# A fifth seven-product block pair in five tiles, strided heads in halves, and a new order of steps and outputs

## The chip, the cores and the metric

The kernel runs on one core of one Trainium2 chip. The metric is the device time of one execution in microseconds (us); for several runs their median is given. The engines are named as in the profile: PE is the matrix engine (TensorE), PEld its weight loads, DVE is VectorE, ACT is ScalarE, POOL is GpSimd, and SP is the queue of SyncE, which here only issues DMAs.

## The reference

Eight heads of sparse attention over 8 batches of 576 tokens; heads 0 to 3 see the last 32 tokens ("local"), heads 4 to 7 see every 32nd token ("strided"). Its output, 4608 tokens of 512 features, goes through a bilinear feed-forward layer.

```python
batch, n_heads, seq, head_dim = (8, 8, 576, 64)
mask_local = (rel >= 0) & (rel < stride)                       # stride = 32
mask_strided = (rel >= 0) & (pos[None, :] % stride == pos[:, None] % stride)
...
attn = np.exp(scores)
attn = attn / (np.sum(attn, axis=-1, keepdims=True) + 1e-09)
attn_out = np.matmul(attn, v)
...
a = x @ w_a            # (4608 x 512) @ (512 x 1536)
b = x @ w_b
return (a * b @ w_out) # (4608 x 1536) @ (1536 x 512)
```

## The kernel before

**Tiles and slots.** The feed-forward layer works on nine tiles of 512 tokens, numbered t = 0 to 8 in the code; tiles "3 to 7" are t = 2 to 6, and these are the ones that the dictionary `MID_A` names. A tile has 16 slots. In slots 0 to 11 the twelve 128-wide blocks f of the hidden layer are made (`a = x @ w_a`, `b = x @ w_b`, product into the buffer `pf`), in slots 12 to 15 ("Y") the output rows. Blocks go in six pairs g = f // 2. A plain block is eight matmuls of 512 columns (four for a, four for b; `ab_mm`, L625), an ACT copy of a out of PSUM (L646) and a DVE multiply with b (L649).

**Pairs by seven products.** For pairs 1 to 4 of t = 2 to 6, `a_pair_mid` computes the a halves of both blocks by seven block products (a 2 x 2 block scheme) in place of eight. Each product is two matmuls of 256 columns (`P`, L695). It needs sums of weights, `wsum_make` (L668, made once), and of inputs, `xsum_make` (L678, once a tile). The order inside a pair is: product 2 into bank Y; product 1 into bank X, which ACT then copies out (`q00`, L721); three of the four matmuls of the second block's b ("b1", L709); product 6 added into X, copied out again (`q10`, L724); product 7 into Z, copied (`p7`, L726); the last b1 matmul; DVE adds Y to `q00` (L717). Here the first half, the even slot, ends. In the odd slot: product 5 added into X, copied (`q11`, L731); product 4 added into Z, DVE adds Z to `q10`; four matmuls of the other b ("b0"); DVE adds `p7` to `q11`; product 3 added into X, copied (`q01`, L738); DVE multiplies both blocks (L714). X is thus written four times and copied four times, and each product on X after the first waits until the copy before it has read the bank. The banks are the four of the rotation `mm_bank` and a fifth, "e"; which of them is X, Y, Z, b1 and b0 follows from (g - 1) % 3.

**Output.** `y_plan` makes the output rows by seven products as well: 84 matmuls of 256 columns (L895), six for each letter and parity in the order `Y_ORDER` (10 11 70 71 ... : product, then token parity 0 or 1). They use three banks X, Y, Z; when a product's second parity ends, `y_post` copies the bank out on ACT (L860) or adds it on DVE. The sums of `pf` that products 3, 5, 6 and 7 read are made by `fast_s` on DVE (L829; n = 0 to 3).

**Attention.** The steps of batch b = t + 1 are put by hand between the matmuls of tile t: `PAIRED` gives steps after a slot, `IN_P` inside the second half of a pair just ahead of the add of `p7`, `IN_Y` after an output product. A step "s4" is the score matmuls of unit 4 into the bank pair `st` (L379) and their exponential on ACT (L399); "m4" is the mask on DVE (L417); "S" is both. "V" is the product with v: for units 0 to 3 (local) L460 with a reciprocal and a multiply on DVE; for units 4 to 7 (strided) `step_VT`: four matmuls into bank "o" and four into "e" (L519), two Ln on ACT (L531), one Exp (L532), two DVE multiplies into `xT` (L534), which is the input of the feed-forward layer. "Q" copies transposed queries (L335), "O" and "I" send rows of the local heads through memory and back, transposed.

**What sets the order.** All five queues are in program order; nothing reorders the instructions. POOL and SP issue the loads and stores; a one-element copy `pace` (L1146) holds POOL's queue to the slots.

Of the kernel before, what the change touches and what calls it, by code (L numbers as in the profile page):

```python
# [7 lines left out]
F32 = mybir.dt.float32  # L8
# [8 lines left out]
RS = 8  # L17
# [8 lines left out]
LV = 80  # L26
WCH = (0, 2, 5, 9, 12)
FAST_Y = (1, 2, 3, 4, 5, 6, 7, 8)
MID_A = {t: (1, 2, 3, 4) for t in (2, 3, 4, 5, 6)}
FAST_A = {7: (1, 2, 3, 4, 5), 8: (0, 1, 2, 3, 4, 5)}  # L30


# [1 line left out]
def kernel(  # L34
# [138 lines left out]
    def fast_w(n, gs):  # L173
        a, b = ((wov[:, 0, 1], wov[:, 0, 0]), (wov[:, 1, 1], wf[:, 0]), (wov[:, 1, 1], wov[:, 0, 1]),
                (wov[:, 1, 0], wf[:, 1]))[n]
        nc.vector.tensor_tensor(wf[:, n, gs], a[:, gs], b[:, gs], op=ALU.subtract)
# [331 lines left out]
    def step_VT(b, u):  # L508

        c, half, M, n, G = unit(u)  # L510
        p = ps.pop((b, u))
        if "e" in psum4:
            o = [psum4[nm].tile([128, 512], F32, tag=nm, name=nm) for nm in "oe"]
        else:
            o2 = psum4["o"].tile([128, 2, 512], F32, tag="o", name="o")
            o = [o2[:, j] for j in range(2)]
        for j in range(2):
            for i in range(G):
                nc.tensor.matmul(o[j][:, i * n:(i + 1) * n], lhsT=vs_buf[b % 2][:, u - HL, 2 * i + j],  # L519
                                 rhs=p_cols(b, p, j, i, n, n)[:M], start=True, stop=True)  # L520
        r = sb.tile([128, RS * 4 * D], BF16, tag="xr", name="xr", bufs=2)[:64, :4 * W].bitcast(F32)
        by_token = lambda t: t.rearrange("d (p i j) -> d p i j", i=G, j=2)
        dst = xT[64 * (u % 2):64 * (u % 2) + 64, c, S * (b % XR):S * (b % XR + 1)]
        if "e" not in psum4:
            by_j = lambda t: t.rearrange("d j (i p) -> d p i j", p=NP)
            nc.scalar.activation(by_token(r), by_j(o2[64:, :, :W]), ACT.Ln)
            nc.scalar.activation(r, r, ACT.Exp, scale=-1.0)
            nc.vector.tensor_mul(by_token(dst), by_j(o2[:64, :, :W]), by_token(r))
            return
        for j in range(2):  # L530
            nc.scalar.activation(by_token(r)[:, :, :, j], o[j][64:, :W].rearrange("d (i p) -> d p i", p=NP), ACT.Ln)  # L531
        nc.scalar.activation(r, r, ACT.Exp, scale=-1.0)  # L532
        for j in range(2):
            nc.vector.tensor_mul(by_token(dst)[:, :, :, j], o[j][:64, :W].rearrange("d (i p) -> d p i", p=NP),  # L534
                                 by_token(r)[:, :, :, j])

    def X_p(b, c):
        x = xn[b, c // 2][:, :, 2 * (c % 2):2 * (c % 2) + 2, :]
# [27 lines left out]
    def F_mm(f, w, kk):  # L566
# [18 lines left out]
    LATER = {-4: "Q0", -3: "Q1", -1: "S0", 0: "S1", 1: "V0", 2: "S2", 3: "V1 Q2 O0", 4: "S3 Q3", 5: "V2", 6: "S4", 7: "V3 O1 I0", 8: "S5", 9: "V4 I1",  # L585
             10: "S6",
             11: "V5"}
    IN_Y = {2: "S7", 6: "V6", 11: "V7"}
    PAIRED = {-4: "Q0", -3: "Q1", -1: "S0", 0: "S1", 1: "V0 Q2", 2: "s2", 3: "V1 Q3 O0", 4: "s3", 5: "V2", 6: "s4", 7: "V3 O1 I0", 8: "s5",
              9: "V4 I1", 10: "s6", 11: "m6 V5"}  # L590
    IN_P = {1: "m2", 2: "m3", 3: "m4", 4: "m5"}
    FN = {"Tk": step_Tk, "Tq": step_Tq, "S": step_S, "V": step_V, "X": step_X, "W": lambda b, n: fast_w(n, slice(0, 3)),
          "s": S_px, "m": S_m, "L": lead_vl, "O": rows_out, "I": rows_in, "Pk": lambda b, c: pair_up("k", c), "Pq": lambda b, c: pair_up("q", c),
          "Q": lambda b, n: step_Q(b, n // 2, n % 2)}

    def run(b, slot):
# [85 lines left out]
    def a_pair_mid(t, g):  # L682
# [10 lines left out]
        def P(bank, lhs, rhs, start=False):  # L693
            for c in range(2):
                nc.tensor.matmul(bank, lhsT=lhs(c), rhs=rhs(c), start=start and c == 0, stop=c == 1, skip_group_check=True)  # L695
# [33 lines left out]
        yield p7[:1, :1]  # L729
        P(X, ws(0), xs(0))  # L730
        nc.scalar.copy(quarter(1, 1), X)  # L731
        P(Z, w(1, 1), xs(3))
        add(quarter(1, 0), Z)
        b_mm(b0, 0, range(KD))
# [3 lines left out]
        nc.scalar.copy(quarter(0, 1), X)  # L738
        mult(1, b1)
        mult(0, b0)  # L740
        if g == 4:
            fast_s(t, 0, slice(0, 4))
        yield pf[:1, 2 * g, :1]

    def a_pair(t, g):
# [73 lines left out]
    def fast_s(t, n, gs):  # L819
        if t not in pss:  # L820
            pss[t] = nat.tile([128, FG * 5 * SW], BF16, tag="shared", name="ps").rearrange("p (n g m) -> p n g m", g=FG, n=5)
        s = pss[t][:, :, gs, :HT]
        x = pfs[t].rearrange("p (g e) (i m) -> p e i g m", e=2, i=2)[:, :, :, gs]
        a, b, op = ((x[:, 0, 1], x[:, 1, 1], ALU.add), (s[:, 0], x[:, 0, 0], ALU.subtract),
                    (x[:, 0, 0], x[:, 0, 1], ALU.subtract), (x[:, 1, 0], s[:, 1], ALU.subtract))[n]
        if (t, n) == (NT - 1, 2) and {gs.start, gs.start + 1} <= set(FAST_A[t]):
            later[t, gs.start] = lambda: nc.gpsimd.tensor_tensor(s[:, n], a, b, op=op)
            return
        nc.vector.tensor_tensor(s[:, n], a, b, op=op)  # L829
# [36 lines left out]
            nc.scalar.copy(part(0, 1), bank)  # L866

    Y_ORDER = [(x[0], int(x[1])) for x in "10 11 70 71 60 61 40 41 50 51 20 21 30 31".split()]
    TAIL_ORDER = [(x[0], int(x[1])) for x in "10 11 20 60 70 61 50 71 30 40 51 41 31 21".split()]

    def by_block(order, lead):
# [8 lines left out]
    def y_plan(t):  # L880

        plan, y = products(t), y_bufs()
        late = t in FAST_A
        if late:
            bank = {x: bank_of(nm, [128, 2, HN]) for x, nm in (("X", "mm"), ("Z", "mm"), ("Y", "tp"))}
        else:
            bank = {x: mm_bank([128, 2, HN]) for x in "ZXY"}

        def store_half(i):
            rows = out[TTOK * t:TTOK * (t + 1)].rearrange("(a i s q) c -> a s i (q c)", i=2, s=8, q=2)  # L890
            nc.sync.dma_start(out=rows[:, :, i], in_=y[i].rearrange("p q c -> p (q c)"))

        for k, q, g in by_block(Y_ORDER, 2 if late else 0):
            b, lhs, rhs = plan[k]
            nc.tensor.matmul(bank[b][:, q], lhsT=lhs(g, q), rhs=rhs(g), start=k in "172" and q == 0 and g == 0,  # L895
                             stop=g == FG - 1, skip_group_check=True)
            if g == FG - 1:
                if q == 1:
                    y_post(k, y, slice(0, 2), bank[b])
                    if k == "5":  # L900
                        y_post("+", y, slice(0, 2), None)
                take(("y", t, Y_ORDER.index((k, q)) + 1))
            yield y
        do(16 * t + 19, store_half, 0)
        do(16 * t + 19, store_half, 1)
# [33 lines left out]
    def ffn_ys(t, j, mid):  # L939
        if j == 0:  # L940
            yst[t] = (y_tail if t == NT - 1 else y_plan)(t)
        for i in range(21):
            y = next(yst[t])
            if i == 10:
                mid()
        if j == 3:
            for _ in yst[t]:
                pass
        return (y[0][:1, 0, :1], None, y[1][:1, 0, HN:HN + 1], y[1][:1, 0, :1])[j]

    def ffn_y(t, j, mid):
        pf = pfs[t]
# [33 lines left out]
    with tc.manual_schedule(engines={ENG.PE, ENG.SP, ENG.Pool, ENG.DVE, ENG.Activation}):  # L986
# [76 lines left out]
        for t in range(NT):  # L1063
            slots += [(ffn_ab, t, f) for f in range(FD)] + [(ffn_ys if t in FAST_Y else ffn_y, t, j) for j in range(4)]
        for b in range(1, B):
            for pos, names in (STEPS.get(b) or {16 * (b - 1) + x: n for x, n in (PAIRED if b - 1 in MID_A else LATER).items()}).items():
                steps.setdefault(pos, []).append((b, names.split()))
            if b not in STEPS:
                for g in MID_A.get(b - 1, ()):
                    steps["p", b - 1, g] = [(b, IN_P[g].split())]  # L1070
                for n, names in IN_Y.items():
                    steps["y", b - 1, n] = [(b, names.split())]

        at = {}

# [2 lines left out]

        soon = {}
        for t in FAST_Y[:-1]:  # L1080
            if t not in FAST_A:
                soon[16 * t + 10] = [lambda t=t: fast_s(t, 2, slice(4, 6))]
            soon[16 * t + 11] = [lambda t=t, n=n: fast_s(t, n, slice(4, 6)) for n in (0, 1)]
# [20 lines left out]
            for (z, nm), g in zip(((0, "k"), (0, "q"), (1, "k"), (1, "q")), gs):  # L1104
                do(g0 + g, step_D, b, z, nm)
        for n in range(4):
            do((17, 17, 18, 19)[n], wsum_make, n, slice(1, 5))
            do(16 * 2 + 12 + n, wsum_make, n, slice(0, 6, 5))
        for t in MID_A:
            do(16 * t - (t > 2), xsum_make, t, 0)  # L1110
            for n in (1, 2, 3):
# [16 lines left out]
                do(16 * (NT - 1) + 2 * g + 1, fast_s, NT - 1, n, slice(g, g + 1))  # L1128
        for t in FAST_Y[:-1]:
            for slot, n, z0, z1 in (  # L1130
                    ((8, 0, 0, 4),) if t == 1 else ()) + ((9, 2, 0, 4), (10, 1, 0, 4), (12, 3, 0, 6)) if t == 1 or t in MID_A else ((4, 0, 0, 2), (5, 2, 0, 2), (6, 1, 0, 2), (7, 3, 0, 2), (8, 2, 2, 4), (9, 0, 2, 4),
                                    (10, 1, 2, 4), (12, 3, 2, 6)):
                do(16 * t + slot, fast_s, t, n, slice(z0, z1))
        for i, (fn, t, j) in enumerate(slots):
# [45 lines left out]
```

## Time and profile before

| | us |
|---|---|
| median of 3 runs (318.65 to 323.52) | 318.68 |
| the profiled execution | 318.67 |
| its span, first to last instruction | 317.0 |
| DVE busy | 263.7 (83%) |
| ACT busy | 198.3 (63%) |
| weight loads (PEld) busy | 220.6 (70%) |
| first output matmul of t = 1, 2, 3, 4, 5, 6, 7 | 80.1, 113.1, 146.0, 179.0, 211.9, 244.8, 274.4 |

The span is cut into instructions of each engine. A matmul's row gives its start and its modelled end; matmuls overlap, so the next one starts before the end of the last, and the distance from start to start is what one costs. A DVE or ACT row ends when its result is there.

### The profile page before, as it was taken

How to read it: one execution, taken by the hardware profiler on the slowest of the kernel's cores; microseconds unless marked ns; L12 is line 12 of the kernel's file. 1: busy time of each engine (PE TensorE's matmuls, PEld its weight loads, DVE VectorE, ACT ScalarE, POOL GpSimd, SP SyncE). 2: the span in 40 equal slices, each digit the busy share in tenths (PEclk: the TensorE clock that was granted, in tenths of full speed). 3: DMA queues.
4: the chain of work that ended last, by engine and by line, in shares of the span. 5: the costliest groups of instructions: out<-in, count | busy, mean ns of one | idle time of the engine just before them, and what ended most of it. 6: DMA issues, size and time to landing. Idle time of an engine off the chain costs nothing. (4 is left out here: it accounts for less than half of the span.)

```text
span 317.0 us, 7353 instructions
## 1 busy us (share of the span) xinstructions
PE 308.2 (97%) x2770; PEld 220.6 (70%) x2798; DVE 263.7 (83%) x594; ACT 198.3 (63%) x414; POOL 112.0 (35%) x186
## 2 busy tenths in 40 slices
PE   7899999999999999999999999999999999999994
PEld 6754565455866687767999986769676966786684
DVE  6887876698979998999799978997899768847862
ACT  7964776455766776567666765686667755435541
POOL 8935712772263164115421434133101112203520
PEclk9999999999999999999999999999999999999999
DMA  9999999999799999999999999899352040004004
GB/s 159 168 205 202 203 184 202 216 104 172 127 137 148 223 144 81 127 228 134 108 114 225 118 130 106 202 138 134 30 154 58 0 135 0 2 0 133 2 0 134
DMA packets 127059, 40.32 MB, mean 127 GB/s; under 512 B 114864, under 2 KB 124144, under 8 KB 126832
## 3 DMA queue, kind: packets, MB, share of 16 engines
q0 software_dynamic: 79760, 19.20, 65.2%
q1 hardware_dynamic: 47120, 20.59, 38.8%
q8 instruction: 22, 0.36, 0.5%
q14 instruction: 13, 0.11, 0.1%
q10 hardware_dynamic: 144, 0.07, 0.1%
HBM read 38.93 MB, written 18.28 MB: 181 GB/s over the span
## 5 line engine op out<-in xcount | busy, mean ns | idle before, releaser
L625 PE MATMUL mm<-xT,wb_sb 128*128 128x512 bf16 (+1 forms) x189 | 46.8, 361 | 0.4
L625 PE MATMUL mm<-xT,wa_sb 128*128 128x512 bf16 (+1 forms) x183 | 46.1, 360 | 0.2
L1146 POOL CAST pace<-pf 1x1 f32<-1x1 bf16 x46 | 14.5, 316 | 81.1 <-DVE pf L714 31.6
L399 ACT ACTIVATE p<-st 72x576 bf16<-72x576 f32 (+1 forms) x56 | 36.4, 650 | 9.1 <-PE st L379 8.2
L709 PE MATMUL mm<-xT,wb_sb 128*128 128x512 bf16 (+1 forms) x160 | 38.0, 342 | 0.4
L646 ACT COPY a_sb<-mm 128x512 f32<-128x512 f32 x44 | 25.7, 583 | 15.7 <-PE mm L625 14.9
L895 PEld LDWEIGHTS <-ps 128*128 128x128 bf16 x336 | 32.7, 98 | 3.7
L625 PEld LDWEIGHTS <-wb_sb 128*128 128x128 bf16 x192 | 18.2, 98 | 16.8 <-DVE pf L714 0.3
L895 PE MATMUL mm<-wf,ps 128*128 128x256 bf16 x252 | 29.8, 273 | 0.0
L860 ACT COPY y_sb<-mm 128x512 f32<-128x512 f32 (+1 forms) x32 | 17.9, 558 | 19.0 <-PE mm L895 16.4
L649 DVE TENSOR_TENSOR pf<-a_sb,mm 128x512 bf16<-128x512 f32 x34 | 23.1, 680 | 5.9 <-ACT a_sb L646 5.8
L625 PEld LDWEIGHTS <-wa_sb 128*128 128x128 bf16 x192 | 17.4, 98 | 12.4
L1146 POOL COPY pace<-y_sb 1x1 f32<-1x1 f32 x22 | 8.4, 380 | 49.9 <-DVE y_sb L858 27.3
L895 PEld LDWEIGHTS <-pf 128*128 128x128 bf16 x252 | 23.5, 98 | 2.7
L775 PE MATMUL mm<-xT,wb_sb 128*128 128x512 bf16 x83 | 25.3, 379 | 0.1
L709 PEld LDWEIGHTS <-wb_sb 128*128 128x128 bf16 x192 | 18.7, 97 | 7.4
L238 POOL DMA_DIRECT2D vs<-in_v_dram x24 | 21.7, 907 | 3.9 <-ACT y_sb L860 1.3
L714 DVE TENSOR_TENSOR pf<-a_sb,mm 128x512 bf16<-128x512 f32 x35 | 22.7, 683 | 0.5
L895 PE MATMUL mm<-wo_sb,pf 128*128 128x256 bf16 x168 | 21.8, 273 | 0.0
L829 DVE TENSOR_TENSOR ps<-pf 128x512 bf16<-128x512 bf16 (+2 forms) x37 | 17.8, 481 | 0.7
L460 PEld LDWEIGHTS <-p 128*128 128x128 bf16 (+1 forms) x256 | 12.9, 97 | 5.2 <-DVE p L417 1.3
L417 DVE TENSOR_TENSOR p<-p,mask_l 128x576 int16<-128x576 int16 x32 | 14.4, 451 | 2.2 <-ACT p L399 2.0
(222 smaller groups left out, 734.2 us busy)
## 6 DMA issues: line engine op xcount, KB each, us to landing
out_dram<-y_sb SPq DMA_DIRECT2D x14, 512.0 KB, 4.8
kr<-in_k_dram POOLq DMA_DIRECT2D x12, 288.0 KB, 6.1
qr<-in_q_dram POOLq DMA_DIRECT2D x12, 288.0 KB, 8.1
vl<-in_v_dram POOLq DMA_DIRECT2D x6, 384.0 KB, 6.9
out_dram<-y_sb SPq DMA_DIRECT2D x7, 256.0 KB, 4.3
vs<-in_v_dram POOLq DMA_DIRECT2D x24, 72.0 KB, 5.7
xd<-xl SPq DMA_DIRECT2D x12, 144.0 KB, 4.0
wo_sb<-in_moe_w_out_dram POOLq DMA_DIRECT2D x4, 384.0 KB, 11.7
```

The lines of the kernel that those rows point to most:

```text
L238: nc.gpsimd.dma_start(out=vs_buf[b % 2][:, h, :, 0:D], in_=v[b, HL + h].rearrange("(p r) d -> p r d", r=RS))
L399: nc.scalar.activation(p_flat(p)[:M, :2 * W].rearrange("p (i n) -> p i n", n=2 * n), st[:M].rearrange("p a (i n) -> p (a i) n", n=256)[:, ...
L625: nc.tensor.matmul(ps_[:, c0:c0 + n], lhsT=w[:, kk, 128 * f:128 * (f + 1)], rhs=xT[:, kk, x0:x0 + n], start=(kk == first and c0 == 0), sto ...
L646: nc.scalar.copy(a_sb, ab[0])
L649: nc.vector.tensor_mul(pf[:, f, :].rearrange("p (i a s) -> p a i s", i=2, s=16), halves(a_sb), halves(ab[1]))
L709: nc.tensor.matmul(dst, lhsT=wb_sb[:, kk, 128 * f:128 * (f + 1)], rhs=rhs, start=kk == 0 and k in (None, 0), stop=kk == KD - 1 and k in (N ...
L714: nc.vector.tensor_mul(pf[:, 2 * g + e, :].rearrange("p (i a s) -> p a i s", i=2, s=16), halves(a[e]), halves(bank))
L775: nc.tensor.matmul(got[e], lhsT=wb_sb[:, kk, 128 * f:128 * (f + 1)], rhs=xT[:, kk, x0:x0 + TTOK], start=kk == 0, stop=kk == KD - 1)
L829: nc.vector.tensor_tensor(s[:, n], a, b, op=op)
L860: nc.scalar.copy({"1": part(0, 0), "7": part(0, 1), "6": part(1, 0), "5": part(1, 1)}[k], bank)
L895: nc.tensor.matmul(bank[b][:, q], lhsT=lhs(g, q), rhs=rhs(g), start=k in "172" and q == 0 and g == 0, stop=g == FG - 1, skip_group_check=True)
L1146: nc.gpsimd.tensor_copy(pace, done)
```

## The change

1. Pair 5 of t = 2 to 6 goes through `a_pair_mid` too (`MID_A`), so blocks 10 and 11 are no longer plain. The weight sums of pair 5 move from t = 2 to t = 1: `wsum_make` takes pairs 1 to 5 and then pair 0, where it took 1 to 4 and then 0 and 5.
2. A strided unit is done in halves. `VT_p` makes four matmuls into one bank ("va", "vb" into "o", "vc" into "e"), one Ln and one Exp of 64 x 288; `VT_n` ("na", "nb") multiplies on DVE later, writing each residue's 72 tokens in turn. Units 4 to 7 are eight such halves, six of them inside Y.
3. Scores of unit 4 move from slot 6 to the end of slot 5, of unit 5 from 8 to 6, of unit 6 from 10 to 7; those of unit 7 stay in Y. Between the halves of pair 4 (after slot 8), after pair 4 (slot 9) and between the halves of pair 5 (slot 10) no step with matmuls is left. "va4" and "vb4" stand inside the second halves of pairs 4 and 5, after product 5.
4. Outputs of these tiles go in `MID_ORDER`; the first three products leave their last matmul (the one on pair 5's blocks) to the end of the group. Steps in Y are placed by matmul number ("m").
5. Sums: n = 0 and n = 3 are made in one piece within Y, n = 1 in one piece from n = 2; the two query copies of the next batch move within Y from matmuls 21 and 42 to 47 and 60.

```diff
-MID_A = {t: (1, 2, 3, 4) for t in (2, 3, 4, 5, 6)}
+MID_A = {t: (1, 2, 3, 4, 5) for t in (2, 3, 4, 5, 6)}
...
+    def VT_p(b, u, h, nm):
+        c, half, M, n, G = unit(u)
+        p = ps[b, u]
+        o = psum4[nm].tile([128, 512], F32, tag=nm, name=nm)
         for j in range(2):
+            for i in range(2):
+                nc.tensor.matmul(o[:, (2 * j + i) * n:(2 * j + i + 1) * n], lhsT=vs_buf[b % 2][:, u - HL, 2 * (2 * h + i) + j],
+                                 rhs=p_cols(b, p, j, 2 * h + i, n, n)[:M], start=True, stop=True)
+        r = sb.tile([128, RS * 4 * D], BF16, tag="xr", name="xr", bufs=2)[:64, :2 * W].bitcast(F32)
+        nc.scalar.activation(r, o[64:, :W], ACT.Ln)
         nc.scalar.activation(r, r, ACT.Exp, scale=-1.0)
+        held[b, "vt", u, h] = o, r
+    def VT_n(b, u, h):
+        o, r = held.pop((b, "vt", u, h))
+        by_j = lambda t: t.rearrange("d (j i p) -> d j i p", j=2, p=NP)
+        dst = xT[64 * (u % 2):64 * (u % 2) + 64, unit(u)[0], S * (b % XR):S * (b % XR + 1)]
+        nc.vector.tensor_mul(dst.rearrange("d (p i j) -> d j i p", i=4, j=2)[:, :, 2 * h:2 * h + 2], by_j(o[:64, :W]), by_j(r))
...
-    PAIRED = {-4: "Q0", -3: "Q1", -1: "S0", 0: "S1", 1: "V0 Q2", 2: "s2", 3: "V1 Q3 O0", 4: "s3", 5: "V2", 6: "s4", 7: "V3 O1 I0", 8: "s5",
-              9: "V4 I1", 10: "s6", 11: "m6 V5"}
+    PAIRED = {-1: "S0", 0: "S1", 1: "V0 Q2", 2: "s2", 3: "V1 Q3 O0", 4: "s3", 5: "s4 V2", 6: "s5", 7: "s6 V3 O1 I0",
+              9: "na4 I1", 11: "nb4"}
     IN_P = {1: "m2", 2: "m3", 3: "m4", 4: "m5"}
+    IN_Q = {4: "va4", 5: "vb4"}
+    IN_Y = {8: "vc5", 12: "s7", 14: "na5 m6", 24: "vb5", 26: "nb5 f0 m7", 34: "vc6", 36: "na6 f3", 44: "vb6", 46: "nb6", 56: "vc7",
+            58: "na7", 67: "vb7", 69: "nb7"}
...
         P(X, ws(0), xs(0))
         nc.scalar.copy(quarter(1, 1), X)
+        take(("q", t, g))
         P(Z, w(1, 1), xs(3))
...
-        if g == 4:
-            fast_s(t, 0, slice(0, 4))
...
+        if n == 1 and t in MID_A:
+            a, b = x[:, 1, 1], s[:, 2]
...
+    MID_ORDER = [(x[0], int(x[1])) for x in "10 11 20 70 71 60 61 40 41 50 51 21 30 31".split()]
...
-        for k, q, g in by_block(Y_ORDER, 2 if late else 0):
+        for m, (k, q, g) in enumerate(by_block(MID_ORDER, 3) if t in MID_A else by_block(Y_ORDER, 2 if late else 0)):
...
+            take(("m", t, m + 1))
...
-            do((17, 17, 18, 19)[n], wsum_make, n, slice(1, 5))
-            do(16 * 2 + 12 + n, wsum_make, n, slice(0, 6, 5))
+            do((17, 17, 18, 19)[n], wsum_make, n, slice(1, 6))
+            do(16 * 2 + 12 + n, wsum_make, n, slice(0, 1))
```

More of the change, by code (lines that the diff above doesn't have):

```diff
@@ L511, in step_VT @@
         p = ps.pop((b, u))
[L512 to L516, printed above, removed]
+        o2 = psum4["o"].tile([128, 2, 512], F32, tag="o", name="o")
+        o = [o2[:, j] for j in range(2)]
         for j in range(2):
@@ L523, in step_VT @@
         dst = xT[64 * (u % 2):64 * (u % 2) + 64, c, S * (b % XR):S * (b % XR + 1)]
[L524 to L529, printed above, removed]
-        for j in range(2):
-            nc.scalar.activation(by_token(r)[:, :, :, j], o[j][64:, :W].rearrange("d (i p) -> d p i", p=NP), ACT.Ln)
-        nc.scalar.activation(r, r, ACT.Exp, scale=-1.0)
-        for j in range(2):
-            nc.vector.tensor_mul(by_token(dst)[:, :, :, j], o[j][:64, :W].rearrange("d (i p) -> d p i", p=NP),
-                                 by_token(r)[:, :, :, j])
+        by_j = lambda t: t.rearrange("d j (i p) -> d p i j", p=NP)
+        nc.scalar.activation(by_token(r), by_j(o2[64:, :, :W]), ACT.Ln)
+        nc.scalar.activation(r, r, ACT.Exp, scale=-1.0)
+        nc.vector.tensor_mul(by_token(dst), by_j(o2[:64, :, :W]), by_token(r))
+    def VT_p(b, u, h, nm):
+        c, half, M, n, G = unit(u)
+        p = ps[b, u]
+        o = psum4[nm].tile([128, 512], F32, tag=nm, name=nm)
+        for j in range(2):
+            for i in range(2):
[3 more added lines that the diff above has]
+        nc.scalar.activation(r, o[64:, :W], ACT.Ln)
+        nc.scalar.activation(r, r, ACT.Exp, scale=-1.0)
+        held[b, "vt", u, h] = o, r
[4 more added lines that the diff above has]
+        nc.vector.tensor_mul(dst.rearrange("d (p i j) -> d j i p", i=4, j=2)[:, :, 2 * h:2 * h + 2], by_j(o[:64, :W]), by_j(r))
     def X_p(b, c):
@@ L584 @@
                  30: "V7"}}
[L585 to L588, printed above, removed]
-    PAIRED = {-4: "Q0", -3: "Q1", -1: "S0", 0: "S1", 1: "V0 Q2", 2: "s2", 3: "V1 Q3 O0", 4: "s3", 5: "V2", 6: "s4", 7: "V3 O1 I0", 8: "s5",
-              9: "V4 I1", 10: "s6", 11: "m6 V5"}
+    PAIRED = {-1: "S0", 0: "S1", 1: "V0 Q2", 2: "s2", 3: "V1 Q3 O0", 4: "s3", 5: "s4 V2", 6: "s5", 7: "s6 V3 O1 I0",
+              9: "na4 I1", 11: "nb4"}
     IN_P = {1: "m2", 2: "m3", 3: "m4", 4: "m5"}
+    IN_Q = {4: "va4", 5: "vb4"}
+    IN_Y = {8: "vc5", 12: "s7", 14: "na5 m6", 24: "vb5", 26: "nb5 f0 m7", 34: "vc6", 36: "na6 f3", 44: "vb6", 46: "nb6", 56: "vc7",
+            58: "na7", 67: "vb7", 69: "nb7"}
     FN = {"Tk": step_Tk, "Tq": step_Tq, "S": step_S, "V": step_V, "X": step_X, "W": lambda b, n: fast_w(n, slice(0, 3)),
-          "s": S_px, "m": S_m, "L": lead_vl, "O": rows_out, "I": rows_in, "Pk": lambda b, c: pair_up("k", c), "Pq": lambda b, c: pair_up("q", c),
+          "s": S_px, "m": S_m, "va": lambda b, u: VT_p(b, u, 0, "o"), "vc": lambda b, u: VT_p(b, u, 0, "e"),
+          "vb": lambda b, u: VT_p(b, u, 1, "o"), "na": lambda b, u: VT_n(b, u, 0), "nb": lambda b, u: VT_n(b, u, 1),
+          "f": lambda b, n: fast_s(b - 1, n, slice(0, FG)), "L": lead_vl, "O": rows_out, "I": rows_in, "Pk": lambda b, c: pair_up("k", c), "Pq": lambda b, c: pair_up("q", c),
           "Q": lambda b, n: step_Q(b, n // 2, n % 2)}
@@ L948, in ffn_ys @@
                 pass
-        return (y[0][:1, 0, :1], None, y[1][:1, 0, HN:HN + 1], y[1][:1, 0, :1])[j]
+        ends = y[1][:1, 0, HN:HN + 1], y[1][:1, 0, :1]
+        return (y[0][:1, 0, :1], None, *(ends[::-1] if t in MID_A else ends))[j]
     def ffn_y(t, j, mid):
@@ L1065 @@
         for b in range(1, B):
-            for pos, names in (STEPS.get(b) or {16 * (b - 1) + x: n for x, n in (PAIRED if b - 1 in MID_A else LATER).items()}).items():
+            t = b - 1
+            for pos, names in (STEPS.get(b) or {16 * t + x: n for x, n in PAIRED.items()}).items():
                 steps.setdefault(pos, []).append((b, names.split()))
             if b not in STEPS:
[L1069 to L1072, printed above, removed]
+                for kind, where in (("p", IN_P), ("q", IN_Q), ("m", IN_Y)):
+                    for x, names in where.items():
+                        steps.setdefault((kind, t, x), []).append((b, names.split()))
+                for x, pos, nm in ((28, 47, "Q0"), (29, 60, "Q1")):
+                    steps.setdefault(("m", t - 1, pos) if t - 1 in MID_A else x, []).append((b, [nm]))
         at = {}
@@ L1080 @@
         for t in FAST_Y[:-1]:
+            if t in MID_A:
+                continue
             if t not in FAST_A:
@@ L1130 @@
             for slot, n, z0, z1 in (
-                    ((8, 0, 0, 4),) if t == 1 else ()) + ((9, 2, 0, 4), (10, 1, 0, 4), (12, 3, 0, 6)) if t == 1 or t in MID_A else ((4, 0, 0, 2), (5, 2, 0, 2), (6, 1, 0, 2), (7, 3, 0, 2), (8, 2, 2, 4), (9, 0, 2, 4),
+                    (8, 0, 0, 4), (9, 2, 0, 4), (10, 1, 0, 4), (12, 3, 0, 6)) if t == 1 else (
+                    (9, 2, 0, 4), (11, 2, 4, 6), (11, 1, 0, 6)) if t in MID_A else ((4, 0, 0, 2), (5, 2, 0, 2), (6, 1, 0, 2), (7, 3, 0, 2), (8, 2, 2, 4), (9, 0, 2, 4),
                                     (10, 1, 2, 4), (12, 3, 2, 6)):
```

## The prediction

> **What bounds the kernel now.** I read the page first, for the busiest engine, then the windows of one tile, then the timeline at the places that the change empties.
>
> ```profile
> PE 308.2 (97%) x2770; PEld 220.6 (70%) x2798; DVE 263.7 (83%) x594; ACT 198.3 (63%) x414; POOL 112.0 (35%) x186
> PEclk9999999999999999999999999999999999999999
> 179.02:211.89 32.87, 32.71 (x290) 23.73 (x290) 29.73 (x67) 22.37 (x49) 11.41 (x19) 1.00 1.38 144
> ```
>
> The last line is t = 4's output start to t = 5's: length, busy PE, PEld, DVE, ACT, POOL, clock, DMA. PE being busy need not mean PE at its rate, so I add up the rate. The chain of waits gives it, and the price of a handover from ACT to PE:
>
> ```profile
> 271.57 0.65 PE mm L775 x3
> ...
> 274.61 9.18 PE mm L895 x84
> ...
> 284.40 0.28 ACT a_sb L784
> 284.69 0.04 issue
> 284.73 0.38 PE ax L768 x2
> ```
>
> A matmul of 512 columns costs 0.65 / 3 = 0.217 us, one of 256 columns 9.18 / 84 = 0.1093. A tile is four plain blocks (32 x 0.217 = 6.93), four pairs (each 8 x 0.217 + 14 x 0.1093 = 3.266; 13.06), 9.18 of outputs, and attention: eight scores at 0.25 (205.90 to 206.15 below), four local products at about 0.19, eight strided half-products at 0.12 to 0.14 (207.66 to 207.92 for two), some 3.8. The sum, 32.97, is the 32.87 measured: in these five tiles PE runs at its rate without a stall, and the list of PE's waits is empty from 80 to 250 us. So every PE saving counts in full, and so does every new PE wait.
>
> **What it saves.** Pair 5's a costs 14 x 0.1093 = 1.530 instead of 8 x 0.217 = 1.733: 0.203 us. t = 4 wraps around the ring of `xT` and its plain a goes in sixteen 256-column matmuls (1.749), so there 0.219. Five tiles: **-1.03 us**. Strided products and scores keep their matmuls, so PE saves nothing else.
>
> **What it uncovers.** The seven products share bank X, and between product 6 and product 5 stands an ACT copy. This is pair 4 of t = 4:
>
> ```profile
> 205.24 0.38 PE L695 MATMUL mm<-xsum,tq 128*128 128x256 bf16 x2
> 205.46 0.38 PE L695 MATMUL e<-xsum,tk 128*128 128x256 bf16 x2
> 205.66 0.37 ACT L724 COPY a_sb<-mm 128x256 f32<-128x256 f32 x1 [0.49 <-PE mm L695]
> 205.68 0.38 PE L709 MATMUL mm<-xT,wb_sb 128*128 128x512 bf16 x1
> 205.90 0.41 PE L379 MATMUL st<-qz0s,kT0s 128*128 128x144 bf16 x4
> 206.15 0.38 PE L695 MATMUL mm<-xsum,tk 128*128 128x256 bf16 x2
> ```
>
> Product 6 starts at 205.24, its copy ends at 206.04, and with the 0.05 of the chain above product 5 may start at 206.09. It starts at 206.15 only because score 5 (205.90 to 206.15) fills the time. The change takes that score away and puts nothing after slot 8: product 5 stands ready at 205.90 and waits **0.19**. Pair 5, after slot 10, has the same shape: **0.19**.
>
> ```profile
> 207.45 0.38 PE L695 MATMUL mm<-xT,tq 128*128 128x256 bf16 x2
> 207.66 0.29 PE L519 MATMUL o<-p,vs 72*128 72x72 bf16 x4
> 207.80 0.29 PE L519 MATMUL e<-p,vs 72*128 72x72 bf16 x4
> 207.86 0.37 ACT L738 COPY a_sb<-mm 128x256 f32<-128x256 f32 x1 [0.61 <-PE mm L695]
> ```
>
> This is pair 4's product 3 and its copy out of bank X, which ends at 208.24. By (g - 1) % 3 X of pair 4 is the third bank of the rotation, which is b1 of pair 5. Pairs 1 and 2 share the same two shapes, but there V1 stands between. After the change nothing does: products 2 and 1 of pair 5 run from 207.66 to 207.66 + 4 x 0.1093 = 208.10, b1 may start at 208.29: **0.19**. In Y, product 3 starts anew in the bank that product 5's copy reads:
>
> ```profile
> 218.96 0.82 PE L895 MATMUL mm<-wo_sb,pf 128*128 128x256 bf16 x6
> 219.16 0.58 ACT L860 COPY y_sb<-mm 128x512 f32<-128x512 f32 x1 [0.81 <-PE mm L895]
> ```
>
> Product 5 ends at 218.96, its copy at 219.74, product 3 may start at 219.79. Before, twelve matmuls lay between; in `MID_ORDER` six and a half unit do, 6 x 0.1093 + 0.125 = 0.78, to 219.74: **0.05**. Sum per tile 0.62, five tiles **+3.1 us**.
>
> **Weight sums.** Pair 5's sums move into t = 1, whose DVE is full: from 59.5 to 71.5 us its only idle moments are of 0.01 to 0.04. There PE already waits for it:
>
> ```profile
> 70.98 0.44 DVE L417 TENSOR_TENSOR p<-p,mask_l 128x576 int16<-128x576 int16 x1
> 71.48 0.36 PE L460 MATMUL o<-vl,p 128*128 128x65 bf16 x6
> ```
>
> Four sums grow from 1024 to 1280 elements; 1024 took 0.69 and 512 took 0.42 (L668), so 256 more cost 0.13: 4 x 0.13 = 0.53 us, all ahead of that mask. Bounds: 0, if the queue had slack that the rows hide, and 0.55. I take **+0.5**, as no row shows slack.
>
> **What lies beside other work.** ACT: five copies of 0.37 replace two of 0.58, and per strided unit two Exps of 288 elements replace one of 576 (0.68); no row shows an Exp of 288, the Ln of the same shape took 0.43, and by it ACT gains 0.7 + 4 x 0.2 = 1.5 us a tile on 22.4 of 32.9. Scores 4 and 6 now put an Exp (0.65) on ACT between a pair's last copy and the next pair's first; counted from product 3's last start it frees ACT at about 1.2, when that copy's bank is ready too (1.19), with 0.02 of slack: 0 to 0.05 at two places a tile, so 0 to +0.5 in all; I take 0. DVE: three adds (0.41) more, two sums merged (0.68 + 0.42 becomes 0.94, twice), so 29.7 becomes about 30.6 in a tile that then lasts 33.3. The halves' multiplies write with a step of eight elements, which no row shows; with a step of two, 288 elements took 0.46 to 0.48, and I take that. By these durations, from the first output matmul on, the two multiplies of pair 5 end at +1.3 (PE needs them at +2.0, after the fifteen matmuls left ahead and two steps), sum n = 1 at +3.0 (+3.6), n = 0 at +5.5 (+6.6), n = 3 at +7.2 (+8.7), the second query copy at +9.4 (S0 needs it at +10.3), nb7 at +10.4 (+11.5). All hidden, by 0.7 or more. Behind nb7, which waits on DVE for its Exp, the add of product 2 and the next tile's first input difference are queued, wanted only by that tile's second block and first pair. vb4 needs na4 off bank "o": 0.25 of cover. The query copies come some 2 to 3 us later, behind them stand only SP's transposes into `qT` for the next batch, half a tile on. O and I keep their slots, no DMA is added; POOL's pace copies keep slots 9 to 12 through the loads that stand there.
>
> **The clock.** The granted clock is 1.00 in all windows, even over the first microseconds, where matmuls were slow (rival 3), so I go by distances: right behind the stall of 0.3 us at 71.5 two matmuls of 512 columns take 0.59 us together, the tail of 0.38 and 0.21 from start to start, the full rate. [...]
>
> **Sum.** 318.67 (span 317.0 and 1.7 around it) - 1.03 + 3.1 + 0.5 = 321.24; the profiled run is the median (318.68). I predict **321.2 us**, 0.8% slower.
>
> **Rivals.** (1) The waits don't come, not slower than before. If ACT's copies were released 0.2 us sooner, product 5 would find its bank free, and -1.03 with 0 to 0.5 for the sums gives 317.6 to 318.2. For it: a wait of 0.19 is no longer than the modelled tail of a matmul (0.38 less 0.217). Against it: product 6 starts 0.07 after the copy q00 ends, never earlier, and 284.40 to 284.73 shows just this handover waited for. (2) DVE becomes the bound in Y. If the stepped writes are slow, say 0.75 (the 576-element multiply of the earlier units, L528) instead of 0.47, five of them stand ahead of the second query copy: 5 x 0.28 = 1.4 against 0.9 of cover, S0 waits 0.5 a tile, 321.2 + 2.5 = 323.7. It decides from 0.47 + 0.9 / 5 = 0.65 us a multiply. Against it: element counts, not steps, order the DVE rows (L534 with its step of two is in line with the add of 256 at 0.41). (3) The PE clock falls after the new waits. At the start twenty matmuls of 224 columns took 3.40 us, 0.17 each, against 0.1093 x 224 / 256 = 0.096 at the rate. One such stretch of 3.4 us a tile loses 3.4 x (1 - 0.096 / 0.17) = 1.5, five 7.4: about 328.6, slower by over 2%. Against it the full rate right behind the stall at 71.5.
>
> **Numbers.** Forecast 0.76 (with its bounds 320.2 to 322.4: without the sums' 0.5 and a wait or two shorter below, the Exps' 0.5 and some more above), rival 1 0.12, rival 2 0.09, rival 3 0.03. The range 318.4 to 323.2 leaves out rival 1 and the upper half of rival 2 with rival 3, under 2 in 10. Two per cent, 6.4 us, is about what a measurement of this kernel tells from no change; only rival 3 goes past it, and no case saves 6 us: faster 0.01, same 0.95, slower 0.04.
>
> **What would show it.** Right: the list of PE's waits in t = 2 to 6, now empty, names ACT copies: `q10` ahead of product 5 in pairs 4 and 5, `q01` ahead of b1 of pair 5, some 0.19 each, and tiles of about 33.3 us from output start to output start; the wait at 71.5 grows to 0.8. Wrong: tiles of 32.7 without waits (rival 1), PE waiting for DVE in Y or at S0 (rival 2), 256-column matmuls further apart than 0.1093 (rival 3).

## The result, and the profile after

The changed kernel takes 352.61 us (median of 5 runs, 351.9 to 356.14) against 318.68: a ratio of 1.110 with a 95% interval of 1.102 to 1.117. The forecast was 321.2, the range ended at 323.2; the kernel is slower by 34 us, not by 2.5.

The profiled run took 355.28 us. In it, between 18 and 24 us, the clock granted to PE was 0.64 (1.00 before), to which I put some 3 us: the first output matmul of t = 1 starts at 83.80 instead of 80.15, and 0.48 of that is longer waits in t = 1. Tiles are therefore compared by their own lengths below. From the page, PE's busy time and clock, and the window of one tile, t = 5's first output matmul to t = 6's (length, busy PE, PEld, DVE, ACT, POOL, clock, DMA):

```profile
PE 318.5 (90%) x2788; PEld 223.4 (63%) x2820; DVE 304.7 (86%) x599; ACT 206.6 (58%) x449; POOL 113.4 (32%) x185
PEclk9879999999999999999999999999999999999999
236.42:275.88 39.46, 34.13 (x292) 24.00 (x294) 38.05 (x68) 23.99 (x56) 5.62 (x12) 1.00 0.65 79
```

The same tile in the kernel before:

```profile
211.89:244.77 32.88, 32.72 (x292) 23.76 (x291) 29.79 (x67) 22.37 (x49) 5.45 (x12) 1.00 0.82 96
```

That tile took 32.88 and takes 39.46, PE is busy 34.1 of it, DVE 38.05: DVE is now the bound. The six lengths from output start to output start, t = 1 on, were 32.95, 32.88, 33.04, 32.88, 32.88, 29.68 and are 33.69, 40.07, 39.44, 39.42, 39.46, 35.13: 32.9 us more, all of it where the changed steps run. What PE waits for there (us in total, times, longest), from the list of PE's waits between 83 and 290 us, and then what DVE does so long, from the page's groups (between the bars busy us and the mean in ns), and last the same multiply in the kernel before (min/median/max in ns):

```profile
PE e L533 <- DVE p L417: 7.0, 5, 1.4
PE o L533 <- DVE xT L545: 6.3, 11, 0.8
PE e L533 <- DVE xT L545: 5.5, 5, 1.1
PE mm L636 <- DVE xT L545: 2.0, 4, 0.7
PE st L379 <- DVE qz0l L335: 1.3, 2, 0.7
PE st L379 <- DVE qz1l L335: 1.3, 2, 0.7
PE e L706 <- ACT a_sb L735: 1.0, 4, 0.2
```

```profile
L545 DVE TENSOR_TENSOR xT<-o,xr 64x288 bf16<-64x288 f32 x25 | 35.9, 1434 | 0.3
L545 DVE TENSOR_TENSOR xT<-e,xr 64x288 bf16<-64x288 f32 x15 | 21.4, 1429 | 0.3
```

```profile
L534 DVE TENSOR_TENSOR xT<-o,xr x20: 470/476/481, 111.0 to 254.3; 64x288 bf16<-64x288 f32 x20
```

L545 is the multiply of `VT_n`. It takes 1.43 us where the same 64 x 288 elements took 0.46 to 0.48 at L534. Eight a tile are 8 x 0.96 = 7.7 us more on an engine that had 3.1 to spare (32.88 less 29.79). One of the waits, on the timeline of DVE and then of PE:

```profile
240.39 1.43 DVE L545 TENSOR_TENSOR xT<-e,xr 64x288 bf16<-64x288 f32 x1
241.85 0.45 DVE L417 TENSOR_TENSOR p<-p,mask_s 72x576 int16<-72x576 int16 x1
```

```profile
240.77 0.27 PE L908 MATMUL mm<-wf,ps 128*128 128x256 bf16 x1
242.46 0.29 PE L533 MATMUL e<-p,vs 72*128 72x72 bf16 x4 [1.41 <-DVE p L417]
```

The list names mask m6 (L417), but the mask takes its usual 0.45. It is na5, queued ahead of it, that keeps DVE till 241.82; PE's half vc6 needs m6, and everything behind vc6 stands from 240.9 to 242.46.

### The profile page after: what moved, and what is told of

It is laid out like the page before. It is cut to its first block, busy times and chain, and to the rows that moved or that the text cites. A ratio compares the mean times of both kernels' runs of the same rounds, so it can differ in the third digit from the quotient of the medians.

```text
span 353.6 us, 7475 instructions
## 1 busy us (share of the span) xinstructions
PE 318.5 (90%) x2788; PEld 223.4 (63%) x2820; DVE 304.7 (86%) x599; ACT 206.6 (58%) x449; POOL 113.4 (32%) x185
## 4 chain that ended last, share of the span: by engine, by line
PE 64%; DVE 23%; issue 7%; DMA 2%; POOL 2%; ACT 1%; POOLq 0%; DVEq 0%
PE mm L636 13%; DVE xT L545 11%; PE mm L908 8%; PE mm L720 8%; PE mm L706 6%; PE mm L785 5%; PE st L379 3%; DVE pf L725 3%; PE mm L972 3%; PE ax L778 3%; PE o L460 2%; DVE ps L841 2%; PE e L706 2%; PE mm L778 2%; DVE p L417 2%
## 5 line engine op out<-in xcount | busy, mean ns | idle before, releaser
L1166 POOL CAST pace<-pf 1x1 f32<-1x1 bf16 x42 | 13.5, 321 | 88.8 <-DVE pf L725 44.5
L636 PE MATMUL mm<-xT,wa_sb 128*128 128x512 bf16 (+1 forms) x135 | 35.9, 366 | 3.1 <-DVE xT L545 2.8
L545 DVE TENSOR_TENSOR xT<-o,xr 64x288 bf16<-64x288 f32 x25 | 35.9, 1434 | 0.3
L908 PEld LDWEIGHTS <-ps 128*128 128x128 bf16 x336 | 31.1, 98 | 5.4 <-DVE ps L841 1.6
L908 PE MATMUL mm<-wf,ps 128*128 128x256 bf16 x252 | 33.0, 273 | 0.2
L657 ACT COPY a_sb<-mm 128x512 f32<-128x512 f32 x34 | 19.8, 584 | 15.9 <-PE mm L636 15.8
L533 PEld LDWEIGHTS <-vs 72*128 72x128 bf16 x160 | 9.6, 97 | 24.5 <-issue 19.9
L908 PE MATMUL mm<-wo_sb,pf 128*128 128x256 bf16 x168 | 23.3, 272 | 0.0
L545 DVE TENSOR_TENSOR xT<-e,xr 64x288 bf16<-64x288 f32 x15 | 21.4, 1429 | 0.3
L636 PEld LDWEIGHTS <-wa_sb 128*128 128x128 bf16 x144 | 13.2, 98 | 10.7 <-issue 0.4
```

The source lines that it names most:

```text
L545: nc.vector.tensor_mul(dst.rearrange("d (p i j) -> d j i p", i=4, j=2)[:, :, 2 * h:2 * h + 2], by_j(o[:64, :W]), by_j(r))
L636: nc.tensor.matmul(ps_[:, c0:c0 + n], lhsT=w[:, kk, 128 * f:128 * (f + 1)], rhs=xT[:, kk, x0:x0 + n], start=(kk == first and c0 == 0), sto ...
L657: nc.scalar.copy(a_sb, ab[0])
L1166: nc.gpsimd.tensor_copy(pace, done)
```

## The experiments

Each run is told with the kernel before on the same chip. Theory A: the multiply is slow because `VT_n` writes residue by residue, one bf16 element and then a step of eight (16 bytes). Rival B: it is the half units, their shape or their place.

**The write order alone undone** (`e1_by_token`).

```diff
-        by_j = lambda t: t.rearrange("d (j i p) -> d j i p", j=2, p=NP)
+        by_j = lambda t: t.rearrange("d (j i p) -> d p i j", j=2, p=NP)
...
-        nc.vector.tensor_mul(dst.rearrange("d (p i j) -> d j i p", i=4, j=2)[:, :, 2 * h:2 * h + 2], by_j(o[:64, :W]), by_j(r))
+        nc.vector.tensor_mul(dst.rearrange("d (p i j) -> d p i j", i=4, j=2)[:, :, 2 * h:2 * h + 2], by_j(o[:64, :W]), by_j(r))
```

> The changed kernel with one edit: VT_n's multiply writes xT token by token (runs of four neighbouring elements) in place of residue by residue (one element, then a step of eight); nothing else. Theory A, the write step of 16 bytes makes the multiply slow: the 40 multiplies fall from 1.43 us to 0.45 to 0.6, PE's waits for DVE in t = 2 to 6 go, and the time falls by about 31 us to the 321 of my sum. Rival B, the multiply is slow for its half-unit shape or the read of PSUM: it stays over 1.2 us and the time over 345.

323.68 us, ratio 1.0149 (1.0106 to 1.0192). The group of the multiply and a tile's window:

```profile
L545 DVE TENSOR_TENSOR xT<-o,xr 64x288 bf16<-64x288 f32 x25 | 15.9, 636 | 0.3
```

```profile
217.68:251.27 33.59, 33.01 (x292) 24.25 (x294) 32.09 (x68) 23.98 (x57) 6.34 (x13) 1.00 0.93 94
```

The edit turns the two reads along with the write, from neighbours to steps of 72 floats and more, and still gives back 29 us; the half units keep their shape and their place. So Theory A stands and B falls. At 0.64 the multiply isn't at 0.47 yet, and PE still waits 0.30 a tile for m6.

**The write order alone done, in the kernel before** (`e2_residue_alone`).

```diff
-            nc.vector.tensor_mul(by_token(dst)[:, :, :, j], o[j][:64, :W].rearrange("d (i p) -> d p i", p=NP),
-                                 by_token(r)[:, :, :, j])
+            nc.vector.tensor_mul(by_token(dst)[:, :, :, j].rearrange("d p i -> d i p"), o[j][:64, :W].rearrange("d (i p) -> d i p", p=NP),
+                                 by_token(r)[:, :, :, j].rearrange("d p i -> d i p"))
```

> The kernel before with one edit: step_VT's two multiplies (t = 2 to 6) run residue by residue, writing with a step of eight elements where it was two. Pairs, scores and order are the old ones. Theory A: each of the 40 multiplies takes about 1.43 us instead of 0.47, DVE needs 29.7 + 8 x 0.96 = 37.4 us in a tile of 32.9, so a tile gets at least 4.5 us longer and the time is 340 to 348. Rival B (it is the half units or their place): under 322.

347.06 us (one run): 28 us slower. Of these, 25.6 lie in the six lengths from output start to output start; another 2.8 lie ahead of them, where the clock was 0.69 between 18 and 24 us. The edit also makes the multiply read the reciprocal with a step of eight floats, which the next run prices by itself. The multiplies and a tile:

```profile
L534 DVE TENSOR_TENSOR xT<-o,xr x20: 1431/1440/1449, 113.8 to 281.7; 64x288 bf16<-64x288 f32 x20
L534 DVE TENSOR_TENSOR xT<-e,xr x20: 1636/1660/1679, 114.9 to 282.7; 64x288 bf16<-64x288 f32 x20
```

```profile
231.40:269.19 37.79, 33.72 (x289) 23.81 (x291) 36.94 (x67) 22.72 (x49) 5.45 (x12) 1.00 0.73 82
```

Durations are min/median/max in ns. DVE is busy 36.9 of 37.8 us. The second of each pair is slower still, 1.66; why wasn't tried.

**The price by itself** (`e3_steps_alone`): behind the kernel before, DVE multiplies of 64 x 288, PSUM f32 times SBUF f32, and copies, each twice; the two repeats agree within 2 ns. The added work makes this run 338.68 us long; from 319 us on no engine but DVE is at work.

```diff
+        for rep in range(2):
+            for st in (1, 2, 4, 8, 16):
+                nc.vector.tensor_mul(big[:64, :288 * st].rearrange("p (n s) -> p n s", s=st)[:, :, 0], a288, b288)
+            for st in (2, 4, 8):
+                nc.vector.tensor_mul(bigf[:64, :288 * st].rearrange("p (n s) -> p n s", s=st)[:, :, 0], a288, b288)
...
```

> The kernel before, and behind it, when all work is done, DVE multiplies of 64 x 288 (PSUM f32 times SBUF f32) that write bf16 with steps of 1, 2, 4, 8, 16 elements, f32 with steps of 2, 4, 8, bf16 in runs of two and four, and two that only read with a step; copies of DVE and ACT with a step. Theory A: the multiply costs 0.47 up to a step of 2 and about 1.43 at 8; whether it rises in proportion to the step (0.8 at 4, 2.7 at 16) or jumps at a fixed distance in bytes is open; runs of four and strided reads stay under 0.6. Rival B: all of them take 0.45 to 0.6.

The rows of single instructions, in ns:

| 288 elements | step 1 | 2 | 4 | 8 | 16 |
|---|---|---|---|---|---|
| DVE multiply writing bf16 | 449 | 470 | 787 | 1422 | 1351 |
| DVE multiply writing f32 | | 451 | 658 | 666 | |
| DVE copy bf16 to bf16 | 227 | | | 797 | |
| ACT copy f32 to bf16 | 428 | 508 | | 1460 | |

bf16 in runs of two or four, then a gap up to eight: 450. Reading SBUF f32 with a step of 8: 656; reading PSUM with a step of 72: 450. So the price neither grows with the step nor jumps once: for bf16 it is 0.47, 0.79 and 1.4 us at 4, 8 and 16 bytes and no more at 32. The 1422 stands with no other engine at work, so the 1.43 in the kernel isn't a matter of what runs beside it. The 0.64 of e1 is then the read of the reciprocal with steps of 72 floats and more, which f1 undoes. My expectation that strided reads stay under 0.6 was a miss.

**The reciprocal in order too** (`f1_reciprocal_by_token`), on e1:

```diff
-        nc.scalar.activation(r, o[64:, :W], ACT.Ln)
+        nc.scalar.activation(r.rearrange("d (p i j) -> d p i j", i=2, j=2), o[64:, :W].rearrange("d (j i p) -> d p i j", j=2, p=NP), ACT.Ln)
...
-        nc.vector.tensor_mul(dst.rearrange("d (p i j) -> d p i j", i=4, j=2)[:, :, 2 * h:2 * h + 2], by_j(o[:64, :W]), by_j(r))
+        nc.vector.tensor_mul(dst.rearrange("d (p i j) -> d p i j", i=4, j=2)[:, :, 2 * h:2 * h + 2], by_j(o[:64, :W]), r.rearrange("d (p i j) -> d p i j", i=2, j=2))
```

> e1 with the order of tokens made one step sooner: the Ln of VT_p reads PSUM by token and writes its result in order, so that the multiply reads it in order too (in e1 it read it with a step of 72 floats and took 0.64). Theory A: multiplies take 0.45, PE's wait of 0.30 a tile for mask m6 behind them on DVE goes, and what is left of my sum is 4 waits of 0.61 a tile on ACT copies, -0.20 saved, and 0.5 in t = 1: tiles of 33.3, 1.5 us less than e1. Rival: the Ln gets as slow as the multiply was or the wait for m6 has another cause: as e1 or more.

321.74 us, ratio 1.0092 (1.0069 to 1.0115); multiplies 0.45, tiles of 33.3. Of the 32.9 us by which the six lengths had grown, 30.7 are gone. The tile from t = 5's output start to t = 6's:

```profile
214.21:247.50 33.29, 32.84 (x292) 24.32 (x294) 30.93 (x68) 23.96 (x57) 6.21 (x13) 1.00 0.94 95
```

With the write step out of the way the rest of the change can be read. Pair 4 of t = 6 and the start of its pair 5, PE and then ACT:

```profile
241.25 0.38 PE L706 MATMUL mm<-xsum,tq 128*128 128x256 bf16 x2
241.47 0.38 PE L706 MATMUL e<-xsum,tk 128*128 128x256 bf16 x2
241.69 0.38 PE L720 MATMUL mm<-xT,wb_sb 128*128 128x512 bf16 x1
242.10 0.38 PE L706 MATMUL mm<-xsum,tk 128*128 128x256 bf16 x2
...
243.75 0.38 PE L706 MATMUL mm<-xT,wa_sb 128*128 128x256 bf16 x2
243.96 0.38 PE L706 MATMUL e<-xT,wa_sb 128*128 128x256 bf16 x2
244.37 0.81 PE L720 MATMUL mm<-xT,wb_sb 128*128 128x512 bf16 x3
```

```profile
241.67 0.37 ACT L735 COPY a_sb<-mm 128x256 f32<-128x256 f32 x1 [0.49 <-PE mm L706]
...
243.95 0.37 ACT L750 COPY a_sb<-mm 128x256 f32<-128x256 f32 x1 [0.15 <-PE mm L706]
```

The b1 matmul of 241.69 is through at 241.91, the copy q10 ends at 242.04, product 5 starts at 242.10: 0.19 lost. Products 2 and 1 are through at 244.18, q01 ends at 244.32, b1 starts at 244.37: 0.19 again. Pair 5's product 5 waits 0.19 as well and product 3 in Y 0.05.

**Scores back between the halves** (`e4_token_scores_back`), on e1:

```diff
-    PAIRED = {-1: "S0", 0: "S1", 1: "V0 Q2", 2: "s2", 3: "V1 Q3 O0", 4: "s3", 5: "s4 V2", 6: "s5", 7: "s6 V3 O1 I0",
-              9: "na4 I1", 11: "nb4"}
+    PAIRED = {-1: "S0", 0: "S1", 1: "V0 Q2", 2: "s2", 3: "V1 Q3 O0", 4: "s3", 5: "V2", 6: "s4", 7: "V3 O1 I0",
+              8: "s5", 9: "na4 I1", 10: "s6", 11: "nb4"}
```

> e1 with scores 4, 5 and 6 back in slots 6, 8 and 10, that is between the halves of pairs 3, 4 and 5. My sum's waits: product 5 of pairs 4 and 5 no longer waits for the copy q10, 2 x 0.19 a tile, five tiles 1.9 us less than e1: about 319.3 if e1 gives 321.2. Rival (the waits of product 5 don't exist or are paid elsewhere): as e1, within 0.4 us.

326.04 us, ratio 1.0209 (1.0166 to 1.0252): a miss, 2.4 us slower than e1. Product 5's waits are gone, but a tile is 33.55 against 33.59: b1 of pair 5 now waits 0.30, vc6 0.45 for its mask (0.30 in e1), va4 0.08. In t = 2, besides, the profiled run lost 2 us as DVE waited for a transposed load:

```profile
DVE qz1s L335 <- DMA qTs<-qr: 2.2, 1, 2.2
```

Why that load landed later than in e1 wasn't tried.

**Cover with scores and a half unit** (`f4_cover`), on f1: the table e4 has, but with score 6 after slot 9 (`9: "s6 na4 I1"`) and `10: "vb4"` in place of `IN_Q`'s. Then **pair 5's weight sums in t = 2** (`f5_cover_sums_late`), on f4:

```diff
-            do((17, 17, 18, 19)[n], wsum_make, n, slice(1, 6))
+            do((17, 17, 18, 19)[n], wsum_make, n, slice(1, 5))
+            do(16 * 2 + 4 + n, wsum_make, n, slice(5, 6))
```

> f1 with matmuls put back into the three empty places: scores 4 and 5 in slots 6 and 8, score 6 after slot 9, the half vb4 after slot 10 (0.125 of 0.19 covered). If my waits are what a tile loses: 0.19 + 0.19 + 0.12 less, tiles of 32.8, five tiles 2.5 us less than f1. Rival, seen in e4: the gain comes back as later waits on DVE or on a longer ACT queue, and the time is within 0.7 us of f1.

> f4 with pair 5's weight sums taken out of t = 1 and made in slots 4 to 7 of t = 2. If the 0.5 of t = 1 was theirs, PE's wait at about 72 us falls from 0.5 back to 0.3 and those behind it likewise, 0.45 us less than f4, and the time is about 0.5 to 1 us under the kernel before (-1.03 saved, 0.25 and 0.3 of waits left). Rival: DVE of t = 2 has no room and PE waits there instead: as f4.

322.31 (ratio 1.0111, 1.0088 to 1.0135) and 322.72 (1.0128, 1.0101 to 1.0154): both miss. In f4 a tile is 33.43, not 32.8. The ACT timeline at pair 5's start shows why:

```profile
243.82 0.37 ACT L750 COPY a_sb<-mm 128x256 f32<-128x256 f32 x1
244.09 0.65 ACT L399 ACTIVATE p<-st 72x576 bf16<-72x576 f32 x1
244.63 0.36 ACT L732 COPY a_sb<-e 128x256 f32<-128x256 f32 x1
```

Score 6 covers q01's copy on PE, but its Exp stands on ACT ahead of the next copy, q00, which ends at 245.00, and product 6 starts 0.16 late at 245.05. In f5 the wait of 0.49 at 67 us that the sums had added is gone, but t = 2 takes 33.67 in place of 33.12: the sums cost on DVE in t = 2 as they did in t = 1.

**Cover without ACT** (`g1_products_reordered`, `g2_sums_on_pool`, `h1_matmul_cover`). g1, on f1, moves product 2 of pairs 4 and 5 behind product 6 and gives pair 5 the banks (2, 4, 1, 0, 3) for Y, X, Z, b1, b0; g2 makes pair 5's sums on POOL in slots 1 to 5 of t = 2; h1 gives pair 4 its old order and puts further matmuls of the pairs ahead of the waits:

```diff
-        b_mm(b1, 1, (0, 1, 2))
+        b_mm(b1, 1, range(3 + (g == 5)))
...
+        if g >= 4:
+            b_mm(b0, 0, (0,))
         P(X, ws(0), xs(0))
```

> f1 with product 2 of pairs 4 and 5 moved behind product 6, and banks of pair 5 changed so that its b1 takes pair 4's Y (free early) and its Y takes pair 4's X. Nothing is put on ACT to cover the copies: 0.22 us of matmul now lies between product 6 and product 5, and b1 no longer waits for the copy q01. If the three waits of 0.19 are what f4 only moved onto ACT's queue: they go, tiles of 32.7 to 32.8 against 33.3 in f1, 2.6 us less than f1, equal to the kernel before within 0.5 us. Rival (f4's): they come back elsewhere, 33.3 or more.

> g1 with pair 5's weight sums made by POOL in slots 1 to 5 of t = 2 in place of DVE in t = 1. If the 0.5 us of t = 1 is DVE's queue: PE's waits at 67 to 74 us fall to those of the kernel before and the time by 0.45 against g1, under the kernel before by 0.3 to 0.8. Rival: POOL's sums hold up its loads, or slow DVE's own operations while both run, and the gain is lost in t = 2.

> g2 with the waits that are left in its tiles (0.05 in Y, 0.13 ahead of pair 4's product 6, 0.03 to 0.06 at three places of pair 5 and behind the halves) covered by the pairs' own matmuls: pair 4 has product 2 in front again, pair 5 does all four b1 matmuls ahead of product 6, and both do the first b0 matmul ahead of product 5. If a tile is the sum of its matmuls once no copy is waited for: 32.88 - 0.20 + 0.05 = 32.73, five tiles 0.7 us under the kernel before, 0.3 us more than g2 would save with its 33.0 (1.4 to 1.6 us less than g2). Rival: the waits move on to other banks and the tiles stay at 33.0.

Ratios 1.0018 (0.9978 to 1.0058), 1.0014 (0.9975 to 1.0054) and 1.0022 (0.9989 to 1.0054); medians 320.39, 320.40 and 319.84 against 320.73 and, for h1, 319.19. From t = 2's output to t = 6's, tiles of about 33.0 in all three (32.9 to 33.5), not the 32.73 that h1 was to reach. In h1 the waits were again others: 0.15 before vc5, 0.16 before pair 5's first b0 matmul, which now comes ahead of the multiply that frees its bank, and the 0.05 in Y; 33.04 less these is 32.68. POOL's sums took the wait in t = 1 back to 0.3, as expected, and the time stayed. Within their intervals these versions are level with the kernel before, though their fastest runs (319.68, 319.68 and 319.69) stay 1.2 to 1.4 us above its fastest on the same chip (318.46 and, for h1, 318.32); none that was tried beats it.

## Why the prediction was wrong

The step that failed is this one: "The halves' multiplies write with a step of eight elements, which no row shows; with a step of two, 288 elements took 0.46 to 0.48, and I take that." The multiply took 1.43. The upper end was wrong too: rival 2 priced a slow multiply at 0.75, from a row with twice the elements and no step in its write, which says nothing of a step. The argument against rival 2, that element counts and not steps order the DVE rows, fell with it: e3 has 449 to 1422 ns at one count. Rival 2 named the right engine and the right point ("from 0.47 + 0.9 / 5 = 0.65 us a multiply"), but with 1.43 in its place DVE isn't late by half a microsecond a tile: 29.7 + 0.9 + 7.7 = 38.3 us of work sets the tile's length, and 38.05 is what the window shows. S0 does wait for the query copy as it said (0.83 us in the tile shown), but as one of several for DVE there, the longest 1.58 ahead of vc6. As no row bounded the price, the range had to be open to the slow side. e1, e2, e3 and f1 settle that this one price is the error: with it undone 30.7 of the 32.9 us that the lengths had grown are gone (f1), brought into the kernel before, with the strided read beside it, it costs 25.6 (e2), and by itself the multiply takes 1.42 (e3).

The other steps, read from f1, where the multiplies take 0.45 as assumed:

- Three waits of 0.19 and one of 0.05 on ACT copies, at the places named: 0.19, 0.19, 0.19, 0.05. By the starts of its matmuls the changed kernel has the three of 0.19 too; the one in Y is covered there, as PE stands 0.80 for DVE just ahead of product 3. Its list of waits counts from a matmul's modelled end, 0.16 after its turn, and so it shows of these only the four of 0.25 at L706 for the copy of L735: pair 5's product 5, where the row of the matmul ahead is missing.
- A tile of 32.87 - 0.20 + 0.62 = 33.29: 33.29 and 33.30. The saving of 0.20 a pair thus stands.
- Weight sums, +0.5 in t = 1: PE's waits there grew from 0.29 to 0.76 in e1, f1 and f4, though as 0.49 at 67 to 70 us and 0.27 some 4.6 us on, not in one place.
- The sum, +2.5: f1 is 2.7 slower than the kernel before on its chip.
- Rival 1 (the waits don't come) fell: they came to the hundredth. Rival 3: PE keeps 0.1093 from start to start and clock 1.00 in the changed tiles, with waits of up to 1.6 us between groups. No run shows the slow stretch of 3.4 us behind a wait that its sum takes: behind the wait of 1.09 that ends at 246.52 ten matmuls of 256 columns take 1.09 from start to start (246.65 to 247.74), 0.109 each.
- Three readings were off without moving the forecast. The rows at 205 to 208 us, put in t = 4, are pair 4 of t = 5. Sum n = 1 had 0.6 of cover (+3.0 against +3.6), not 0.7. And the tail of a matmul, 0.38 less 0.217, is 0.16, so a wait of 0.19 is longer than it, which takes from rival 1 its one argument.

What I would have said of any fix was wrong as well: f4 was to gain 2.5 us and gained none.

## What to carry to other kernels

When an instruction's access pattern changes, its duration is unknown until a row has the same element size and the same step in bytes: at one step of 16 bytes DVE's write of 288 elements took 1422 ns in bf16 and 658 in f32 (e3). Measure it first, and don't bound it by rows with other element counts. Writing single bf16 elements with a step of 8 or 16 bytes cost 1.75 and 3.2 times the dense write here (787 and 1422 ns against 449); order the loops so that at least two neighbours are written in a run (450), and let the strided side be the read from PSUM (450 with a step of 72 floats). Where PE waits for a copy, cover it with matmuls that bring no new work to the engine that copies: that took tiles from 33.3 to 33.0 us here (f1 to g1), while a score that brings an Exp moved the wait to the next copy (f4, 33.43).

## What the runs showed of the hardware

A write of 288 bf16 elements cost DVE 449 ns dense and 1422 ns at a step of 16 bytes, and ACT 428 and 1460; the same step in bytes cost DVE 658 with f32 elements, and runs of two bf16 at the same spacing cost no more than the dense write (450). At a step of 8 bytes bf16 took 787, so the widest step that was all but free here is 4 bytes for bf16 (470) and 8 for f32 (451, beside the 449 of dense bf16). What sets these prices wasn't shown. Also not expected: in four of the twelve profiled runs, of versions of both kernels (the changed kernel, e1, e2 and g1), the clock granted between 18 and 24 us was 0.62 to 0.75 (0.64 in the changed kernel; over the whole of these runs 0.988 to 0.995), in the other eight 1.00. What sets it off wasn't tried.
